# Even frequencies of a folded sequence transform split into four groups

## The chip, the cores and the metric

The program runs on one core of one Trainium2 chip. A core has several engines that run their own instruction streams and meet through semaphores: TensorE (PE: matmuls and transposes; PEld is its loading of weights), VectorE (DVE), ScalarE (ACT), GpSimd (POOL) and SyncE (SP, here the engine that issues most DMAs). Matmuls write PSUM banks; the other engines read these and return them. All data are fp32 unless said otherwise. The metric is the device time of one execution in microseconds, median of several; lower is better. A profiled execution is a separate one.

## What is computed

Four batches go through attention and then through a Fourier mixing block with an MLP:

```python
batch, n_heads, seq, head_dim = (4, 8, 768, 64)
# attention, per head
q_bucket = sum of 6 sign bits of q @ proj          # k_bucket likewise
scores = scale * q @ k^T, -1e9 where q_bucket != k_bucket
attn_out = softmax(scores) @ v
x = attn_out.transpose(0, 2, 1, 3).reshape(B, S, H * D)   # (4, 768, 512)
# Fourier mixing and MLP, per batch
X = fft(fft(x, axis=1), axis=2); mixed = real(X)
u = x + mixed
un = (u - mean(u)) / sqrt(var(u) + 1e-6)           # over the 512 channels
out = u + relu(un @ w_ch1) @ w_ch2                 # 512 -> 2048 -> 512
```

Only the real part of the two-dimensional transform over 768 positions and 512 channels is wanted, so cosines and sines are enough, and both can be halved by symmetry: adding and subtracting mirrored entries ("folding") separates even from odd frequencies, and cosine from sine terms.

## The kernel before

**Two interleaved generators.** `attention(b)` and `mix(b)` are Python generators. `mix` of batch b-1 is stepped inside `attention(b)`: after every attention step the main loop calls `next(other)` until the count of steps done keeps up with `(MIX - LEFT)` steps in all, spread over the 24 steps of attention (`while done * steps < (MIX - LEFT) * (i - wait)`, L1611). What is left of a mix runs ahead of the next attention; `mix(3)` runs alone at the end. By the profile `mix(0)` takes from about 130 to 350 us, `mix(1)` 350 to 610, `mix(2)` 610 to 870 and `mix(3)` 904 to the end. Only the first part of the program (up to the end of `attention(0)`) is emitted in a fixed order; afterwards the tile framework's scheduler decides the order of instructions on every engine, from priorities, program order and its own estimates of when operands are ready. Helpers bend it: `in_turn` and `done_by` tie an instruction behind the latest noted one of an engine, `behind` ties a matmul to the matmul before it and lifts it.

**Attention.** A pair of heads n (four pairs per batch) has six chunks c of 128 keys. Scores `sc` (L905, two 64-row matmuls of 384 columns per half g) go into two double-bank PSUM buffers ("sc"); ScalarE takes the exponential into one of two `pk` buffers (L916); VectorE multiplies `pk` by the mask "bucket of q equals bucket of k" (L930, from `qb` and `kb`); TensorE multiplies by values into `oo` (L941); VectorE adds `pk` into `acc` (L1037, 1536 columns, two chunks one after the other every second step), which is what is left of a chunk's `pk` besides `oo`. At the end of a pair `scale` sums `acc` over keys on TensorE (L951), spreads the reciprocals with eight small ScalarE copies (L984), a VectorE transpose (L989) and multiplies (L993), giving `x`. `prepare(n + 1)` makes `qt` and `kt` (VectorE transposes, L779), the bits (L836, L840) and `qb`, `kb` (L850, L860, evacuated at L535, L537 and L864), and `load` fetches q, k, v through SP.

**The transform in `mix`.** `fold` (L1110) works on a channel half `cp`: for each parity `pc` of channel frequencies it forms e = x of one half plus or minus x of the other (L1118, 768 columns), f = first plus or minus second half of the sequence for `par` 0 (even) and 1 (odd) sequence frequencies (L1123), and z, four additions of f to itself mirrored, for both `par` at once (L1132), with a copy of two special columns (L1136). z has 384 rows for each `par`, ordered cosine rows, both special ones, sine rows. `fold(b, 0)` runs inside `attention(b)`, in the last pair; `fold(b, 1)` begins `mix(b)`.

Then come six `cs` tiles (L1158), three of 128 rows for each `par`, which transform the channels: a tile takes only cosine or only sine channel products (256 or so columns in all, written to PSUM with stride 2 for the two `pc`), the middle tile both. ScalarE copies them into F (L1165, L1171, the latter mirrored). Then, per block j of 128 channels, the products A and B (L1187): for each `par`, `k` 0 and 1 (cosine into A, sine into B), two matmuls t accumulate over two 128-row tiles of F with the constant `sq` into 193 or 192 columns. VectorE adds or subtracts A and B to and from x in four additions of 384 columns (L1201), which return the two PSUM banks.

**The MLP in `mix`.** Both products run as seven-product (Strassen-like) schemes: sums t1, t2, t4, t3 of blocks of x (L1445, L1446, L1447, L1452) and of the weights; `un` transposes of x (L1213) for the residual and the norm; inner products `h_p` (L1467), with combinations of weights fetched through SP into a ring from `ad` (L1440); outer products `o` (L1346) with weights `bd` refetched by quarters (L1351), and VectorE additions from PSUM (L1358, L1392 to L1398). The weights' combinations `ad` and `bd` are written to DRAM during `mix(0)` (L1266, L1317), through SP. Results are stored at L1096.

**PSUM.** Besides the two double-bank "sc" and the two "o" buffers of attention there are two banks "ps". `pt` (L520) gives `mix` its banks: only those two, except at the start and once attention is over (`roomy`), when it also uses the "o" and "sc" buffers, six in all.

Of the kernel before, what the change touches and what calls it, by code (L numbers as in the profile page):

```python
# [49 lines left out]
def _consts():  # L50


    s = np.arange(HALF)
    freq = np.concatenate([2 * np.arange(NK), 2 * np.arange(NK) + 1])
    ang = 2.0 * np.pi * (np.outer(s, freq) % S) / S
    seq = np.stack([np.cos(ang), np.sin(ang)])
    seq = seq.reshape(2, NT // 2, P, 2 * NK).transpose(2, 0, 1, 3)


    d = np.arange(DM // 2)  # L60
    ang = 2.0 * np.pi * (np.outer(d, np.arange(DM)) % DM) / DM
    sin = -np.sin(ang)
    sin[0] = 1.0 - 2.0 * (np.arange(DM) % 2)
    chan = np.concatenate([np.cos(ang), sin]).reshape(NDC, P, DM).transpose(1, 0, 2)

    off = np.zeros((P, 2))
    for h in range(2):
        off[h * D : h * D + NBITS] = 0.5  # L70
        off[h * D + NBITS] = (NBITS / 4.0, -1.0)


    pw = np.zeros((P, 2, P))
    for r in range(P):
        h, bit = divmod(r % 32, NBITS)
        if h < 2:
            pw[r, h] = 2.0**bit


    d = np.arange(DM // 2)
    fr = np.concatenate([np.arange(DM // 2 + 1), np.arange(1, DM // 2)])
    ang = 2.0 * np.pi * (np.outer(d, fr) % DM) / DM
    ch = np.where(np.arange(DM) <= DM // 2, np.cos(ang), np.sin(ang))
    ch = ch.reshape(2, P, DM // 2, 2).transpose(1, 0, 3, 2)

    s = np.concatenate([np.arange(2, HALF // 2, 2), np.arange(1, HALF // 2, 2)])  # L90
    rows = np.concatenate([s, [0, HALF // 2], s])
    kind = np.repeat([0, 1, 2, 3], [len(s), 1, 1, len(s)])
    sq = np.zeros((2, 2, P, HALF + 1))
    for par in range(2):
        cols = slice(par * NK, HALF + 1 if par else NK)
        ang = 2.0 * np.pi * (np.outer(rows, freq[: HALF + 1][cols]) % S) / S
        for k in range(2):
            own = kind == (0 if par == k else 3)
            own |= (kind == 1) & (k == 0) | (kind == 2) & (k == par)
            w = np.where(own[:, None], np.sin(ang) if k else np.cos(ang), 0.0)  # L100
            w = w.reshape(NT // 2, P, -1)
            sq[0, k, :, cols] = w[0 if par == k else 2]
            sq[1, k, :, cols] = w[1]
    sq = sq.transpose(2, 0, 1, 3)
    return {
        "pw": np.ascontiguousarray(pw, dtype=np.float32),
        "ch": np.ascontiguousarray(ch, dtype=np.float32),
        "sq": np.ascontiguousarray(sq, dtype=np.float32),
        "seq": np.ascontiguousarray(seq, dtype=np.float32),
        "chan": np.ascontiguousarray(chan, dtype=np.float32),  # L110

        "off4": np.ascontiguousarray(np.tile(off[:32], (4, 1)), dtype=np.float32),
        "own": np.ascontiguousarray(
            np.where(np.arange(P)[:, None] // 32 % 2 == np.arange(2), BIG, 0.0),
            dtype=np.float32,
        ),
        "off": np.ascontiguousarray(off, dtype=np.float32),
    }
# [367 lines left out]
def _main(  # L486
# [616 lines left out]
    def turned(ap, first, n):  # L1103

        at = ap[tuple([slice(None)] * (len(ap.shape) - 1) + [slice(first, first + 1)])]
        return bass.AP(at.tensor, at.offset, [*[list(d) for d in at.ap[:-1]], [-1, n]])

    def fold(b, cp):


# [4 lines left out]
        for pc in range(2):  # L1115
            ef = wt([P, 2, S], F32, "ef", f"ef{b}_{cp}_{pc}", 1)
            e = ef[:, 0]
            nc.vector.tensor_tensor(  # L1118
                e, x[:, cp], x[:, cp + 2], op=ALU.subtract if pc else ALU.add
            )  # L1120
            f = ef[:, 1].rearrange("p (r n) -> p r n", r=2)
            for par in range(2):
                nc.vector.tensor_tensor(  # L1123
                    f[:, par], e[:, 0:HALF], e[:, HALF:S],
                    op=ALU.subtract if par else ALU.add,
                )
            z = zs[b][:, cp, pc]
            n = HALF // 4 - 1
            for at, op in ((0, ALU.add), (2 * n + 3, ALU.subtract)):

                for i, first, last in ((0, 1, n), (n, 2 * n + 2, n + 1)):
                    nc.vector.tensor_tensor(  # L1132
                        z[:, :, at + i : at + i + last], f[:, :, first : first + last],
                        turned(f, 2 * n + 1 if i == 0 else HALF - 1, last), op=op,
                    )
            nc.vector.tensor_copy(  # L1136
                z[:, :, 2 * n + 1 : 2 * n + 3], f[:, :, 0 : n + 2 : n + 1]
            )
            yield

    def mix(b):
# [5 lines left out]
        hd = DM // 2  # L1147
        F = wt([P, 2, 2, 2, DM], F32, "F", f"F{b}", 1)
        nc.gpsimd.memset(F[:, :, 1, :, 0 : hd + 1 : hd], 0.0)
        for par in range(2):  # L1150
            for t in range(NT // 2):
                ps = pt([P, DM], f"cs{b}_{par}_{t}")
                kinds = (0, 1) if t == 1 else (par ^ (t // 2),)
                for pc in range(2):
                    lo = 0 if 0 in kinds else hd // 2 + 1 - pc
                    hi = hd if 1 in kinds else hd // 2 + 1 - pc
                    for cp in range(2):
                        nc.tensor.matmul(  # L1158
                            ps[:, pc + 2 * lo : pc + 2 * hi - 1 : 2],
                            z[:, cp, pc, par, t * P : (t + 1) * P],  # L1160
                            ch[:, cp, pc, lo:hi], start=(cp == 0), stop=(cp == 1),
                        )
                f = F[:, par, :, t % 2]
                for k in kinds:
                    done_by[ET.Activation] = nc.scalar.copy(  # L1165
                        f[:, k, k : hd + 1 - k],
                        ps[:, k * (hd + 1) : DM if k else hd + 1],
                    )
                f = f[:, kinds[0] : kinds[-1] + 1, hd + 1 :]
                r = ps[:, (kinds[0] + 1) * hd - 1 : (kinds[0] + 1) * hd]  # L1170
                nc.scalar.copy(  # L1171
                    f,
                    bass.AP(
                        r.tensor, r.offset, [r.ap[0], [hd, len(kinds)], [-1, hd - 1]]
                    ),
                )
                yield

        for j in range(NDC):
            pa, pb = (pt([P, HALF + 1], f"{nm}{b}_{j}") for nm in "AB")
            for par in range(2):
                cols = slice(par * NK, HALF + 1 if par else NK)
                for k, ps in enumerate((pa, pb)):
                    for t in range(2):
                        nc.tensor.matmul(  # L1187
                            ps[:, cols], F[:, par, k, t, j * P : (j + 1) * P],
                            sq[:, t, k, cols], start=(t == 0), stop=(t == 1),
# [2 lines left out]
            for ps, op in (pa, ALU.add), (pb, ALU.subtract):  # L1192
                for i in range(2):
# [8 lines left out]
                        u, u, f, op=op if (j < 2) ^ i else ALU.add  # L1202
                    )
            yield

        yield from mlp7(b)

# [388 lines left out]
    for b in range(B):  # L1596
        if b > 0:
# [9 lines left out]
            for i, _ in enumerate(attention(b), 1):  # L1607
                if b == 1 and i == 2:
                    for f, avg in means:
                        centre(f, avg)  # L1610
                while done * steps < (MIX - LEFT) * (i - wait):  # L1611
                    next(other)
                    done += 1
        if b == B - 1:
# [75 lines left out]
```

## Time and profile before

| what | value |
| --- | --- |
| time, median of 3 runs | 1075.66 us (1075.48 to 1076.36) |
| profiled execution, its own time | 1079.48 us |
| span of the profiled execution | 1077.7 us, granted TensorE clock 0.994 of full |
| cs, groups in batches 1 to 3 | 3 tiles of 128 rows per `par` |
| A and B, even half, per batch | 16 matmuls of 193 columns, two records each |
| DMA | 103.13 MB, 96 GB/s over the span |

The profiled execution takes 3.8 us longer than the median of the others, so its parts are compared with its own time. The span runs from its first to its last instruction. The page gives busy time by engine over the whole span, the span in 40 slices, the chain of work that ended last, and groups of instructions by line, engine and operation. An fp32 matmul shows as two records, so "x4965" counts records. In a timeline line the columns are the start in us, the duration, engine, line, operation, output and inputs, shapes, how many in a row were joined, and in brackets the idle time ahead of it and what ended that. "Step" below is the time from one record's start to the next one's on the same engine while it is busy; it is shorter than a record's own duration, which overlaps with its neighbours.

### The profile page before, as it was taken

To read this page: it belongs to the slowest core of one execution; us is meant where nothing else is said; L and a number is where in the kernel's file an instruction comes from. 1 tells how busy PE (TensorE), PEld (TensorE's weight loads), DVE (VectorE), ACT (ScalarE), POOL (GpSimd) and SP (SyncE) were. 2 spreads that over 40 slices of the span, in tenths; PEclk is the share of its full clock that TensorE was granted. 3 is DMA by queue.
4 is the path that set the end of the run, shared out by engine and by line. 5 is a ranking of instruction groups with operands and counts; after the bars stand their busy time and mean duration, and the time that the engine had idled before them with its cause. 6 is when DMAs were issued, how large, how long until landed. Compare 5 with 4: busy or idle time off the path is not lost.

```text
span 1077.7 us, 14180 instructions
## 1 busy us (share of the span) xinstructions
PE 1037.1 (96%) x4965; PEld 634.2 (59%) x4965; DVE 779.9 (72%) x1328; ACT 500.0 (46%) x1055; POOL 59.1 (5%) x132
## 2 busy tenths in 40 slices
PE   7999899999999999999999999999999999999997
PEld 3333364447644585545664575645675579668576
DVE  5788969896799977777858876776856875644353
ACT  6888554662287414455335424454325522440420
POOL 0000000011000020010000020010000012100000
PEclk9999999999999999999999999999999999999999
DMA  8764551370154461224062233222033205222301
GB/s 202 202 139 88 103 140 48 122 231 15 26 131 170 135 180 45 52 64 88 10 191 75 64 102 118 50 65 69 15 112 94 69 23 173 60 79 91 124 20 42
DMA packets 175710, 103.13 MB, mean 96 GB/s; under 512 B 129552, under 2 KB 162960, under 8 KB 175632
## 3 DMA queue, kind: packets, MB, share of 16 engines
q1 hardware_dynamic: 169840, 88.65, 30.5%
q0 software_dynamic: 4224, 13.11, 3.9%
q8 instruction: 41, 0.67, 0.2%
q10 hardware_dynamic: 1568, 0.39, 0.2%
q14 instruction: 37, 0.30, 0.1%
HBM read 81.14 MB, written 20.97 MB: 95 GB/s over the span
## 4 chain that ended last, share of the span: by engine, by line
PE 77%; DVE 12%; ACT 6%; issue 2%; SPq 1%; DMA 1%; ACTq 0%; DVEq 0%
PE o L1346 26%; PE h_p L1467 22%; PE oo L941 10%; PE sc L905 9%; PE cs L1158 3%; ACT pk L916 2%; DVE pk L930 2%; PE A L1187 2%; DVE acc L1037 2%; PE B L1187 1%; PE sum L951 1%; SPq L576 1%; DVE x L1201 1%; PE bits L836 1%; DMA kn<-in_k_dram 1%
## 5 line engine op out<-in xcount | busy, mean ns | idle before, releaser
L1346 PE MATMUL o<-w,h 128*128 128x256 f32 x1152 | 260.1, 383 | 0.8 <-DVE w L1358 0.5
L1346 PEld LDWEIGHTS o<-w,h 128*128 128x128 f32 x1152 | 217.8, 191 | 41.7 <-issue 6.4
L916 ACT ACTIVATE pk<-sc 128x768 f32<-128x768 f32 x192 | 147.1, 807 | 80.0 <-PE oo L941 34.7
L1467 PE MATMUL h_p<-x,w 128*128 128x384 f32 x448 | 165.4, 497 | 3.1 <-ACT w L1534 1.7
L905 PE MATMUL sc<-qt,kt 64*128 64x384 f32 x768 | 153.9, 503 | 3.1 <-ACT pk L916 2.8
L930 DVE SCALAR_TENSOR_TENSOR pk<-qb,kb,pk 128x768 f32<-128x768 bf16 x132 | 128.7, 1012 | 38.4 <-ACT pk L916 38.3
L941 PE MATMUL oo<-pk,vn 128*64 128x385 f32 (+1 forms) x768 | 146.2, 495 | 0.8 <-DVE pk L930 0.6
L1467 PEld LDWEIGHTS h_p<-x,w 128*128 128x128 f32 x448 | 82.4, 190 | 69.3 <-issue 9.8
L1467 PE MATMUL h_p<-w 128*128 128x384 f32 x288 | 106.1, 490 | 0.1
L1037 DVE TENSOR_TENSOR acc<-acc,pk 128x1536 f32<-128x1536 f32 (+1 forms) x64 | 98.5, 1549 | 5.4 <-ACT pk L916 5.2
L941 PEld LDWEIGHTS oo<-pk,vn 128*64 128x64 f32 x768 | 50.5, 136 | 86.3 <-issue 72.8
L905 PEld LDWEIGHTS sc<-qt,kt 64*128 64x128 f32 x768 | 66.3, 186 | 55.9 <-issue 19.0
L1467 PEld LDWEIGHTS h_p<-w 128*128 128x128 f32 x288 | 53.6, 190 | 39.6 <-ACT w L1522 2.4
L1376 ACT COPY tq<-o 128x256 f32<-128x256 f32 x24 | 8.9, 372 | 105.0 <-PE o L1346 105.0
L1358 DVE SCALAR_TENSOR_TENSOR w<-o,rs,w 128x256 f32<-128x256 f32 x56 | 26.6, 479 | 41.2 <-PE o L1346 41.2
L1481 ACT ACTIVATE h<-h 128x384 f32<-128x384 f32 x72 | 37.4, 524 | 24.6 <-DVE h L1523 10.5
L1346 PE MATMUL o<-w 128*128 128x256 f32 x176 | 42.2, 383 | 0.2 <-DVE w L1358 0.2
L1518 DVE TENSOR_TENSOR h<-h 128x384 f32<-128x384 f32 x32 | 17.8, 555 | 29.7 <-ACT h L1517 29.7
L1096 POOL DMA_DIRECT2D out_dram<-w x30 | 16.3, 547 | 407.6 <-issue 314.6
L1346 PEld LDWEIGHTS o<-w 128*128 128x128 f32 x176 | 32.9, 190 | 7.5 <-DVE w L1358 1.2
L1365 ACT COPY tq<-o 128x256 f32<-128x256 f32 x24 | 8.8, 368 | 60.1 <-PE o L1346 59.9
L1392 DVE TENSOR_TENSOR tq<-tq,o 128x256 f32<-128x256 f32 x24 | 10.0, 417 | 36.4 <-PE o L1346 36.4
(169 smaller groups left out, 1317.4 us busy)
## 6 DMA issues: line engine op xcount, KB each, us to landing
w<-ad SPq DMA_DIRECT2D x168, 128.0 KB, 2.0
w<-bd SPq DMA_DIRECT2D x42, 512.0 KB, 4.4
zraw<-in_moe_w_ch_dram POOLq DMA_DIRECT2D x16, 512.0 KB, 3.9
bd<-w SPq DMA_DIRECT2D x14, 512.0 KB, 4.4
vn<-in_v_dram SPq DMA_DIRECT2D x32, 192.0 KB, 3.3
qn<-in_q_dram SPq DMA_DIRECT2D x120, 48.0 KB, 2.4
kn<-in_k_dram SPq DMA_DIRECT2D x60, 96.0 KB, 3.1
zraw<-in_moe_w_ch_dram SPq DMA_DIRECT2D x8, 512.0 KB, 6.9
```

The lines of the kernel that those rows point to most:

```text
L905: last[0] = nc.tensor.matmul(ps[:, h, 0:HALF], kt[rows, ks], qt[rows, qs], start=kb is not None, stop=True,)
L916: done_by[ET.Activation] = nc.scalar.activation(pk[:, g, :, 0:HALF], ps[:, :, 0:HALF], AF.Exp, scale=SCALE)
L930: done_by[ET.DVE] = nc.vector.scalar_tensor_tensor(w, qb[:, h].rearrange("p (g s) -> p g s", g=2), kb[:, h, c : c + 1], w, op0=ALU.is_equa ...
L941: oo = nc.tensor.matmul(oos[g][h * D : (h + 1) * D, 0:w], nat["v", n][:, (2 * c + h) * D : (2 * c + h + 1) * D], pk[:, g, h, 0:w], start=( ...
L1037: done_by[ET.DVE] = nc.vector.tensor_tensor(acc[:, g], (first if c == 1 else acc)[:, g], new[:, g], op=ALU.add,)
L1158: nc.tensor.matmul(ps[:, pc + 2 * lo : pc + 2 * hi - 1 : 2], z[:, cp, pc, par, t * P : (t + 1) * P], ch[:, cp, pc, lo:hi], start=(cp == 0) ...
L1187: nc.tensor.matmul(ps[:, cols], F[:, par, k, t, j * P : (j + 1) * P], sq[:, t, k, cols], start=(t == 0), stop=(t == 1),)
L1346: nc.tensor.matmul(ps, a[:, r], right7[i][:, r], start=start and r == 0, stop=r == HF // 2 - 1, skip_group_check=not start,)
L1358: nc.vector.scalar_tensor_tensor(t[:, cols], src, r, t[:, cols], op0=ALU.mult, op1=ALU.add)
L1467: nc.tensor.matmul(ps, left[:, k], right[i][:, k], start=start and k == 0, stop=k == 1, skip_group_check=not start,)
L1481: done_by[ET.Activation] = nc.scalar.activation(h, h, AF.Relu)
L1518: done_by[ET.DVE] = nc.vector.tensor_tensor(c22, c21, c22, op=ALU.add)
```

## The change

For batches 1 to 3 the even frequencies (`par` 0) are folded once more. Frequency 2m over 768 positions is frequency m over 384; these split again into even m and odd m. z for `par` 0 then consists of four groups of 97, 96, 96 and 95 rows, beginning at rows 0, Q + 1, 2Q + 1 and 3Q + 1 (Q = 96): cosine rows for even m and for odd m, sine rows for odd m and for even m. `refold` makes them from f in two VectorE additions of 384 columns, eight of 94 to 96 columns written through interleaved access patterns, and one small copy; the old fold then handles `par` 1 alone, with four additions and a copy of its own.

The `cs` tiles of `par` 0 become four, of 97, 96, 96 and 95 rows. None of them needs both kinds of channel products. In A and B, for `par` 0, each pair of accumulating 193-column matmuls becomes two single ones: group t has its own 97 or 96 frequencies, contracts over 95 to 97 rows, and writes every second column of the same 193 columns of PSUM. Odd frequencies and the VectorE additions at L1201 stay.

The constant for it, `sq2`, is loaded over the even columns of `sq` after batch 0's A and B, which still use the old one, by a DMA on SP. The step count of a mix rises by the extra tile: `MIX + (b > 1)`, the mix that attention(2) or attention(3) steps.

```diff
+    even, odd = 2 * np.arange(1, HALF // 8), 2 * np.arange(HALF // 8) + 1
+    pairs = np.concatenate([even, odd])
+    sq2 = np.zeros((P, 2, 2, NK))
+    for k, rest, rows in (
+        (0, 0, np.concatenate([[0], pairs, [HALF // 4]])),
+        (0, 1, np.concatenate([[0], pairs])),
+        (1, 1, np.concatenate([[HALF // 4], pairs])),
+        (1, 0, pairs),
+    ):
+        ang = 2.0 * np.pi * (np.outer(rows, np.arange(rest, NK, 2)) % HALF) / HALF
+        sq2[: len(rows), rest, k, : ang.shape[1]] = np.sin(ang) if k else np.cos(ang)
...
+    Q = HALF // 4
+
+    def refold(z, f, spare):
+
+        h = spare[:, 0:HALF].rearrange("p (s r n) -> p s r n", s=2, r=2)
+        g = f.rearrange("p (r h n) -> p h r n", r=2, h=2)
+        for i, op in ((0, ALU.add), (1, ALU.subtract)):
+            nc.vector.tensor_tensor(h[:, i], g[:, 0], g[:, 1], op=op)
+        for op, first, step in ((ALU.add, 1, 2 * Q + 1), (ALU.subtract, 3 * Q + 1, -2 * Q + 1)):
+            for r, i0, n in ((0, 1, Q // 2 - 1), (1, 0, Q // 2)):
+                a, d = h[:, 0, r, i0 : i0 + 1], first + (Q // 2 - 1) * r
+                d = z[:, d : d + 1]
+                nc.vector.tensor_tensor(
+                    bass.AP(d.tensor, d.offset, [list(d.ap[0]), [step, 2], [1, n]]),
+                    h[:, :, r, i0 : i0 + n],
+                    bass.AP(
+                        a.tensor, a.offset + Q - 1 - i0,
+                        [list(a.ap[0]), [2 * Q, 2], [-1, n]],
+                    ),
+                    op=op,
+                )
+        nc.vector.tensor_copy(
+            bass.AP(z.tensor, z.offset, [list(z.ap[0]), [Q + 1, 2], [Q, 2]]),
+            h[:, :, 0, 0 : Q // 2 + 1 : Q // 2],
+        )
...
+            if b > 0:
+                refold(z[:, 0], f[:, 0], e)
+                z, f = z[:, 1:2], f[:, 1:2]
...
+        tiles = [
+            (par, t * P, P, (0, 1) if t == 1 else (par ^ (t // 2),), t % 2)
+            for par in range(2) for t in range(NT // 2)
+        ]
+        if b > 0:
+            tiles[0:3] = (
+                (0, 0, Q + 1, (0,), 0), (0, Q + 1, Q, (0,), 1),
+                (0, 2 * Q + 1, Q, (1,), 1), (0, 3 * Q + 1, Q - 1, (1,), 0),
+            )
+        for t, (par, z0, m, kinds, slot) in enumerate(tiles):
+            ps = pt([P, DM], f"cs{b}_{par}_{t}")[0:m]
...
-                            z[:, cp, pc, par, t * P : (t + 1) * P],
+                        z[:, cp, pc, par, z0 : z0 + m],
...
+                        if b > 0 and par == 0:
+                            m = Q + 1 - t if k == 0 else Q - 1 + t
+                            nc.tensor.matmul(
+                                ps[:, t:NK:2], F[0:m, 0, k, t, j * P : (j + 1) * P],
+                                sq[0:m, t, k, 0 : Q + 1 - t], start=True, stop=True,
+                            )
+                            continue
                         nc.tensor.matmul(
                             ps[:, cols], F[:, par, k, t, j * P : (j + 1) * P],
                             sq[:, t, k, cols], start=(t == 0), stop=(t == 1),
...
+        if b == 0:
+            nc.sync.dma_start(sq[:, :, :, 0:NK], cn["sq2"].ap())
...
-                while done * steps < (MIX - LEFT) * (i - wait):
+                while done * steps < (MIX + (b > 1) - LEFT) * (i - wait):
```

More of the change, by code (lines that the diff above doesn't have):

```diff
@@ L108, in _consts @@
         "sq": np.ascontiguousarray(sq, dtype=np.float32),
+        "sq2": np.ascontiguousarray(sq2, dtype=np.float32),
         "seq": np.ascontiguousarray(seq, dtype=np.float32),
@@ L1149, in mix @@
         nc.gpsimd.memset(F[:, :, 1, :, 0 : hd + 1 : hd], 0.0)
[L1150 to L1159, printed above, removed]
-                            z[:, cp, pc, par, t * P : (t + 1) * P],
[L1161 to L1167, printed above, removed]
-                    )
[L1169 to L1175, printed above, removed]
-                )
-                yield
@@ new lines, in mix @@
+        tiles = [
[9 more added lines that the diff above has]
+            ps = pt([P, DM], f"cs{b}_{par}_{t}")[0:m]
+            for pc in range(2):
+                lo = 0 if 0 in kinds else hd // 2 + 1 - pc
+                hi = hd if 1 in kinds else hd // 2 + 1 - pc
+                for cp in range(2):
+                    nc.tensor.matmul(
+                        ps[:, pc + 2 * lo : pc + 2 * hi - 1 : 2],
+                        z[:, cp, pc, par, z0 : z0 + m],
+                        ch[:, cp, pc, lo:hi], start=(cp == 0), stop=(cp == 1),
+                    )
+            f = F[0:m, par, :, slot]
+            for k in kinds:
+                done_by[ET.Activation] = nc.scalar.copy(
+                    f[:, k, k : hd + 1 - k],
+                    ps[:, k * (hd + 1) : DM if k else hd + 1],
+                )
+            f = f[:, kinds[0] : kinds[-1] + 1, hd + 1 :]
+            r = ps[:, (kinds[0] + 1) * hd - 1 : (kinds[0] + 1) * hd]
+            nc.scalar.copy(
+                f,
+                bass.AP(
+                    r.tensor, r.offset, [r.ap[0], [hd, len(kinds)], [-1, hd - 1]]
+                ),
+            )
+            yield
@@ L1186, in mix @@
                     for t in range(2):
+                        if b > 0 and par == 0:
+                            m = Q + 1 - t if k == 0 else Q - 1 + t
+                            nc.tensor.matmul(
+                                ps[:, t:NK:2], F[0:m, 0, k, t, j * P : (j + 1) * P],
+                                sq[0:m, t, k, 0 : Q + 1 - t], start=True, stop=True,
+                            )
+                            continue
                         nc.tensor.matmul(
```

## The prediction

> **What bounds the kernel now.** I read the page's busy times, then the windows by stage, then the groups by form, then the timelines around the transform. Page, first part:
>
> ```profile
> PE 1037.1 (96%) x4965; PEld 634.2 (59%) x4965; DVE 779.9 (72%) x1328; ACT 500.0 (46%) x1055; POOL 59.1 (5%) x132
> ```
>
> TensorE works for 96% of the span. Of the 40.6 us without a matmul, some 24 lie in the first 130 us and the closing stores. So removed TensorE time is worth its full length, except where another engine releases TensorE. The windows (us, then PE, PEld, DVE, ACT, POOL busy) show where that is:
>
> ```profile
> 610.00:653.00 43.00, 43.00 (x206) 33.59 (x206) 30.96 (x63) 10.15 (x29) 7.12 (x15) 1.00 0.45 128
> 653.00:674.00 21.00, 20.73 (x124) 11.67 (x123) 16.79 (x19) 12.00 (x24) 1.60 (x3) 1.00 0.15 47
> 674.00:696.00 22.00, 19.83 (x121) 14.66 (x120) 15.69 (x26) 6.09 (x14) 0.00 (x0) 1.00 0.32 54
> 911.00:922.00 11.00, 11.00 (x72) 10.98 (x71) 7.41 (x15) 1.30 (x4) 0.00 (x0) 1.00 0.01 1
> ```
>
> 674 to 696 is the second half of batch 2's transform (products A and B, transposes `un`), run inside batch 3's attention: TensorE loses 2.17 us there. At 400 to 445 batch 1 does the same. 911 to 922 is batch 3's, which has no attention beside it: no loss. TensorE's own timeline shows the owner of the losses:
>
> ```profile
> 678.63 1.54 PE L1187 MATMUL A<-sq,F 128*128 128x193 f32 x8 [0.68 <-DVE x L1201]
> ...
> 689.63 1.54 PE L1187 MATMUL A<-sq,F 128*128 128x193 f32 x8 [0.55 <-DVE x L1201]
> ...
> 693.59 0.77 PE L1213 MATMUL un<-ident,x 128*128 128x128 f32 x5 [0.70 <-DVE x L1201]
> ```
>
> VectorE's four additions per channel block (L1201) return the PSUM banks of A and B. Batches 1 and 2 have two banks for this, batch 3 six. VectorE's timeline after them:
>
> ```profile
> 692.51 1.02 DVE L1201 TENSOR_TENSOR x<-x,B 128x384 f32<-128x384 f32 x2 [0.28 <-PE B L1187]
> 693.45 1.75 DVE L1037 TENSOR_TENSOR acc<-acc,pk 128x1536 f32<-128x1536 f32 x1
> 695.12 0.95 DVE L1446 TENSOR_TENSOR w<-x,w 128x768 f32<-128x768 f32 x1
> 695.98 1.75 DVE L1037 TENSOR_TENSOR acc<-acc,pk 128x1536 f32<-128x1536 f32 x1
> ```
>
> Every L1201 comes ahead of the two long sums L1037.
>
> [...] back-to-back 128-column loads of `cs` step 111 to 112 ns whether 127, 128 or 129 columns stream, against 162 ns for 192 or 193 and 216 for 256. [...] `cs` writes every second column and its 256 columns still step 216 ns, as the contiguous `o` products do. I price stride 2 at nothing.
>
> **The change part by part.**
>
> *A and B, even half.* Each fp32 matmul is two records. Per channel block 4 matmuls of 193 columns become 4 of 97 or 96: 8 x 162.5 = 1.30 us become 8 x 112 = 0.90. Gain 0.40 per block, 1.6 per batch, 4.8 over 12 blocks. [...]
>
> *cs.* Three tiles, 8 x 111.5 + 8 x 216 + 8 x 111.5 = 3.51 us, become four of 8 x 110 = 3.52 us: nothing. Each of the four is evacuated by two ScalarE copies (0.27 + 0.38 us and 0.2 us of signal) while the next runs 0.88 us on the second bank: up to 0.1 us twice in batches 1 and 2. The lone extra ACT copy per batch is covered by ScalarE's idle time (46% busy); uncovered it is 0.4.
>
> *Fold.* Of this the trace has the old form: L1132, 190 or 192 columns, steps 0.27 us; 384 steps 0.47. That gives 0.065 us plus N/0.96 each. Old tail per (channel half, parity): 4 x 0.27 + 0.07 = 1.15. New: 2 x 0.27 + 8 x 0.165 + 2 x 0.07 = 2.0. Plus 0.87, 3.5 us of VectorE per batch. In batches 2 and 3 it lies under `o` products; batch 3's z is complete at 893.3 against its first use at 904.28, 11 us of cover for 1.7. Without cover it would cost 3.5. Bounds on the unseen interleaved writes: 0.165 and twice that, 1.3 us more a batch, still covered.
>
> *The new constant's load* (395 KB, SP queue) waits until batch 0's A and B are read, at about 171; behind it stand the `ad` stores, used 240 us later. It needs the next quarter's buffers only microseconds later than now. Nothing[...].
>
> *Order, batch 1 before cs.* The compiled order puts batch 2's first scores behind the last `o` products. That removes these waits (ScalarE's 8 small copies stood ahead of the exponential):
>
> ```profile
> 372.77 0.92 PE L905 MATMUL sc<-qt,kt 64*128 64x384 f32 x4 [0.27 <-ACT pk L916]
> 375.27 0.97 PE L905 MATMUL sc<-qt,kt 64*128 64x384 f32 x4 [1.59 <-ACT pk L916]
> ```
>
> Minus 1.86. But VectorE is full from 350 to 376 (34.3 of 36 us). Walking it with the refold added, the L1358 that frees the next `o` bank stands behind L989, which waits for those 8 copies, and ends near 375.3, 1.0 us after TensorE wants the bank. Also 0.3 for a score wait and cs. Net -0.6. Some q and k loads move behind the seven `bd` loads; their users come 4 us or more later.
>
> *Order in A and B, batches 1 and 2.* Two things change. VectorE now has L1037, half of A3's additions, L1037, the other half, B3's: before, A3, B3, L1037. And TensorE has the next scores, the first `oo` group and the transposes interleaved ahead of the first MLP product. I walk batch 2 from its first A product (674.67 now), 0.2 us from matmul to addition and 0.15 back. VectorE: A0 and B0 done at 4.8, kt 5.8, A1 6.7, B1 11.1, A2 12.2, L1445 13.1, B2 14.0, L1037 15.7, L1037 again 17.9 (half of A3 between), A3 18.3, B3 19.3, then L930, L1446, L930 to 22.0 and, with L1447, the second chunk's to 24.7. TensorE: A0, qb, B0, kb, score, A1, score to 6.0, `oo` 8.7, B1 9.9, A2 11.0, B2 (0.27 lost) 12.4, A3 13.5, B3 (0.7 lost) 15.3. The next score needs a PSUM buffer that the exponential frees, which must wait for L1037 to finish with `pk`: 16.6, 1.3 lost. Transposes 18.4; `oo` waits for L930 until 22.1, 1.0 lost; MLP at 26.6. Now the same work, less the 9.4 us of MLP, sums and other transposes done by 711.3, takes 36.65 - 9.4 = 27.2. Batch 2 gains 0.6, less 0.2 for cs. In batch 1, A1's second half stands behind `oo`: 0.65 later, gain 0, less 0.2. Of 3.2 us that the two batches' matmuls save, 0.6 is left.
>
> *Batch 3.* TensorE 2.2 us per block, additions 1.9: still TensorE's. Copies of the last cs tile are 0.15 late. Gain 1.6, but L1445 and L1446, which the second MLP product needs, now follow all additions: ready at 12.25 from the first A product, TensorE there at 11.7. It stands at 13.7 now with 0.1 us less done: gain 1.5.
>
> Sum: batch 1 -0.6 - 0 + 0.2, batch 2 -0.4, batch 3 -1.5: -2.3. Profiled execution: 1079.48, of it 1077.7 span, so 1077.2. It stands 3.8 above the median of 1075.66[...]; the same difference on the median gives **1073.4**, 0.21% less.
>
> **Rivals.** *All of it arrives* (1069.5): 4.8, batch 1's 1.9 whole, minus 0.5. For it: 96% busy, and work pulled ahead in one stage leaves VectorE ahead in the next. Against: three of the four waits in the stage are VectorE's already. *VectorE takes over, slower* (1079): if the pair of L1037 ahead of B3's additions delays score and `oo` by 1.5 us more than walked in both batches, and the first fold in batch 1, on a full VectorE, passes its 1.7 us on, 3 + 1.7 - 2.3 + 0.9 of waits at moved qb copies gives +3.3. It decides once the losses of the stage, 2.2 now, exceed about 4.5 per batch. *The matmuls do not shorten* (1078): a short matmul costs 162 as before, and the added orders lose 2. Against: `cs` steps 112.
>
> **How the numbers follow.** The walked case 0.45, all of it 0.27, VectorE 0.2, no shortening 0.08. 0.2% (2.15 us) is about what a measurement of this kernel can tell from no change. The walk is good to 1.5 us: half of it falls beyond 0.2% faster. Faster 0.27 + 0.23 = 0.50; same 0.22 + 0.03 = 0.25; slower 0.25. The walked case alone 1071.9 to 1075.5; the range, 8 in 10, from all of it to the lighter half of VectorE's case: 1069.3 to 1078.6.
>
> **What would show it.** A and B records of 97 columns stepping 112 ns; 96 `z` additions of 94 to 96 columns at 0.25 us; no wait of 1.59 near 375; in batches 2 and 3's common stage, waits of about 1.3 (score, on an exponential behind L1037) and 1.0 (`oo`, on L930); batch 3's cs to first MLP product about 1.5 shorter. I am wrong if 97 columns step 82 or 160, if z holds up cs, or if those waits are absent or twice as long.

## The result, and the profile after

The changed kernel takes 1081.33 us (median of 6 runs, 1080.64 to 1082.82) against 1076.13 us before: a ratio of 1.0043, 95% interval 1.0032 to 1.0054. The forecast was 1073.4, with a range of 1069.3 to 1078.6. The time rose instead of falling.

TensorE's busy time fell, as the page's first part of the changed kernel shows, and VectorE's rose by about the 10 us that the new folds were costed at:

```profile
PE 1034.6 (96%) x4989; PEld 628.8 (58%) x4989; DVE 790.1 (73%) x1412; ACT 499.7 (46%) x1058; POOL 63.9 (6%) x132
```

The windows of the changed kernel (us, then PE, PEld, DVE, ACT, POOL busy, granted clock, DMA share, GB/s), first those that answer to the prediction's, then two of the MLP's second half of batches 1 and 2:

```profile
610.00:653.00 43.00, 43.00 (x206) 33.46 (x205) 32.36 (x77) 10.17 (x28) 7.16 (x15) 1.00 0.44 123
653.00:674.00 21.00, 20.73 (x132) 11.79 (x131) 16.73 (x19) 12.10 (x25) 1.56 (x3) 1.00 0.15 57
674.00:696.00 22.00, 20.35 (x123) 13.58 (x124) 18.32 (x29) 8.24 (x16) 0.00 (x0) 0.92 0.35 54
911.00:922.00 11.00, 11.00 (x83) 10.79 (x82) 5.15 (x11) 3.02 (x10) 0.54 (x1) 1.00 0.12 44
...
550.00:610.00 60.00, 58.77 (x238) 28.59 (x238) 45.70 (x81) 30.84 (x65) 0.00 (x0) 1.00 0.35 93
800.00:870.00 70.00, 68.65 (x288) 38.61 (x288) 49.83 (x90) 32.59 (x67) 0.00 (x0) 1.00 0.32 99
```

The last two, in the kernel before:

```profile
550.00:610.00 60.00, 59.95 (x251) 30.64 (x251) 45.03 (x69) 32.03 (x66) 0.00 (x0) 1.00 0.39 104
800.00:870.00 70.00, 69.95 (x290) 40.01 (x289) 50.61 (x79) 32.67 (x67) 0.44 (x1) 1.00 0.30 94
```

The common stage of batch 2 (674 to 696) has no more idle time than it had (1.65 us against 2.17), though its granted clock of 0.92 makes some records longer (the score pairs at 691.91 and 692.55 step 0.64 us, where 0.32 is usual). What is new is where TensorE had been fully busy: 1.2 us idle in 550 to 610 and 1.4 in 800 to 870, between MLP products. TensorE's timeline of the changed kernel names who was late:

```profile
574.62 1.56 PE L1526 MATMUL h_p<-x,w 128*128 128x384 f32 x4 [0.60 <-ACT h L1576]
...
594.33 1.56 PE L1526 MATMUL h_p<-w 128*128 128x384 f32 x4 [0.62 <-ACT w L1593]
...
689.03 0.66 PE L1238 MATMUL B<-sq,F 95*128 95x97 f32 x4 [0.46 <-DVE x L1257]
...
691.45 2.60 PE L918 MATMUL sc<-qt,kt 64*128 64x384 f32 x8 [1.09 <-ACT pk L929]
...
852.43 1.56 PE L1526 MATMUL h_p<-w 128*128 128x384 f32 x4 [1.30 <-ACT w L1593]
```

The waits at 689 and 691 are those that the prediction walked to (VectorE on a bank, then a score on an exponential). Those at 574, 594 and 852 are ScalarE's copies of `h_p` that return MLP banks, and nothing in the prediction stands for them. VectorE in the common stage has the walked order: half of A3's additions (L1257, L1201 of before) between the two long sums into acc (L1050, L1037 of before), the other half behind the second, and B3's last:

```profile
688.80 1.75 DVE L1050 TENSOR_TENSOR acc<-acc,pk 128x1536 f32<-128x1536 f32 x1
690.47 0.54 DVE L1257 TENSOR_TENSOR x<-x,A 128x384 f32<-128x384 f32 x1
690.94 1.75 DVE L1050 TENSOR_TENSOR acc<-acc,pk 128x1536 f32<-128x1536 f32 x1
692.61 0.54 DVE L1257 TENSOR_TENSOR x<-x,A 128x384 f32<-128x384 f32 x1
693.07 1.00 DVE L1257 TENSOR_TENSOR x<-x,B 128x384 f32<-128x384 f32 x2
```

For where the time went, the trace is cut at each batch's first A product. The three stretches behind batch 1's first A product hold all the rest of the kernel; times in us, from the traces of all kernels that ran, the ratio with its 95% interval. "Idle" is TensorE's idle time in the first and the second stretch. "Shapes" counts, in the same two, how often TensorE goes over to a stationary operand of another shape: 64 rows for scores, 64 columns for `oo`, 32 rows or columns for `qb`, `kb`, `bits` and `sum`, 95 to 128 of both for the transform and the MLP.

| kernel | A of 1 to A of 2 | A of 2 to A of 3 | A of 3 to last matmul | idle | shapes | ratio to before |
| --- | --- | --- | --- | --- | --- | --- |
| before | 254.73 | 236.63 | 158.76 | 2.96, 2.70 | 84, 67 | |
| changed | 259.24 | 239.84 | 156.34 | 5.86, 4.50 | 88, 67 | 1.0043 (1.0032 to 1.0054) |
| e1, step count undone | 255.49 | 236.87 | 156.34 | 4.82, 4.55 | 79, 61 | 0.9978 (0.9967 to 0.9989) |
| e2, step count alone | 257.44 | 236.91 | 158.75 | 5.35, 3.78 | 83, 64 | 1.0027 (1.0019 to 1.0034) |
| e3, VectorE's fold alone | 256.25 | 238.17 | 158.75 | 4.02, 3.75 | 84, 67 | 1.0016 (1.0009 to 1.0023) |
| e4, batch 3 alone | 254.71 | 238.40 | 156.34 | 2.96, 3.81 | 84, 67 | 0.9988 (0.9977 to 0.9999) |
| e5, e1 with GpSimd | 255.56 | 236.93 | 156.34 | 4.82, 4.55 | 79, 61 | 1.0008 (1.0000 to 1.0016) |
| e6, short matmuls alone | 252.52 | 234.42 | 157.10 | 2.39, 2.12 | 84, 67 | 0.9949 (0.9934 to 0.9964) |
| e7, batches 2 and 3 | 257.07 | 236.88 | 157.10 | 4.07, 4.56 | 86, 61 | 1.0018 (1.0011 to 1.0025) |
| e8, one step fewer than e1 | 256.36 | 237.76 | 156.34 | 4.82, 4.56 | 81, 63 | 1.0007 (0.9999 to 1.0015) |
| e9, steps aligned | 254.41 | 236.21 | 156.34 | 3.70, 3.43 | 84, 67 | 0.9959 (0.9945 to 0.9973) |
| e10, e9 with GpSimd | 256.94 | 237.29 | 156.34 | 4.76, 4.50 | 84, 67 | 0.9995 (0.9987 to 1.0004) |
| e11, e9, half the fold later | 253.35 | 234.97 | 156.34 | 2.44, 2.11 | 86, 69 | 0.9948 (0.9935 to 0.9962) |
| e12, e9, all of it later | 256.77 | 236.18 | 156.34 | 4.51, 2.90 | 84, 69 | 0.9977 (0.9971 to 0.9984) |

So the change gains 2.42 us in batch 3 and loses 4.51 and 3.21 in the two batches before: +5.3, the size of the measured 5.2. In the traced execution of before the granted clock fell to 0.5 in two stretches of 3.4 us, from 205.3 and from 376.0. e4's code is the same up to batch 1's first A product but for line numbers; its trace has no such stretch and is 3.35 us ahead at that mark (416.59 against 419.94). That is most of the 3.8 us by which the profiled execution stood above the median. Against e4, the changed kernel is 0.6 us shorter from batch 0's first A product to batch 1's (266.6 against 267.2). Other traces have one such stretch too: e5 from 205.1, e10 from 590.7, e12 from 606.9 (in the last two it is worth up to 1.7 us of their first column, half of e4's difference), and the changed kernel from 691.8, where it seems to have cost little, since two executions of it at a granted clock of 0.999 took 1081.24 and 1081.49.

### The profile page after: what moved, and what is told of

It is laid out like the page before. It is cut to its first block, busy times and chain, and to the rows that moved or that the text cites. A ratio compares the mean times of both kernels' runs of the same rounds, so it can differ in the third digit from the quotient of the medians.

```text
span 1079.1 us, 14329 instructions
## 1 busy us (share of the span) xinstructions
PE 1034.6 (96%) x4989; PEld 628.8 (58%) x4989; DVE 790.1 (73%) x1412; ACT 499.7 (46%) x1058; POOL 63.9 (6%) x132
## 4 chain that ended last, share of the span: by engine, by line
PE 73%; DVE 15%; ACT 6%; issue 2%; DMA 1%; SPq 1%; DVEq 0%; ACTq 0%
PE o L1405 25%; PE h_p L1526 20%; PE oo L954 10%; PE sc L918 9%; PE cs L1207 3%; DVE pk L943 3%; DVE acc L1050 2%; ACT pk L929 2%; PE sum L964 1%; PE A L1243 1%; ACT rr L997 1%; PE un L1272 1%; PE B L1243 1%; DVE x L1257 1%; DMA kn<-in_k_dram 1%
## 5 line engine op out<-in xcount | busy, mean ns | idle before, releaser
L1526 PE MATMUL h_p<-x,w 128*128 128x384 f32 x448 | 164.1, 493 | 4.4 <-ACT h L1566 1.8
L954 PE MATMUL oo<-pk,vn 128*64 128x385 f32 (+1 forms) x768 | 149.0, 496 | 1.6 <-DVE pk L943 1.3
L1526 PEld LDWEIGHTS h_p<-x,w 128*128 128x128 f32 x448 | 82.2, 190 | 70.5 <-issue 8.1
L1526 PE MATMUL h_p<-w 128*128 128x384 f32 x288 | 106.4, 490 | 2.0 <-ACT w L1593 1.9
L1050 DVE TENSOR_TENSOR acc<-acc,pk 128x1536 f32<-128x1536 f32 (+1 forms) x64 | 98.5, 1548 | 5.4 <-ACT pk L929 5.2
L1526 PEld LDWEIGHTS h_p<-w 128*128 128x128 f32 x288 | 53.3, 190 | 41.2 <-ACT w L1593 4.4
L1417 DVE SCALAR_TENSOR_TENSOR w<-o,rs,w 128x256 f32<-128x256 f32 x56 | 26.5, 478 | 36.4 <-PE o L1405 36.4
```

The source lines that it names most:

```text
L954: oo = nc.tensor.matmul(oos[g][h * D : (h + 1) * D, 0:w], nat["v", n][:, (2 * c + h) * D : (2 * c + h + 1) * D], pk[:, g, h, 0:w], start=( ...
L1050: done_by[ET.DVE] = nc.vector.tensor_tensor(acc[:, g], (first if c == 1 else acc)[:, g], new[:, g], op=ALU.add,)
L1417: nc.vector.scalar_tensor_tensor(t[:, cols], src, r, t[:, cols], op0=ALU.mult, op1=ALU.add)
L1526: nc.tensor.matmul(ps, left[:, k], right[i][:, k], start=start and k == 0, stop=k == 1, skip_group_check=not start,)
```

## The experiments

Two theories stood against each other: that the shift of attention against the mix (one more step, `MIX + (b > 1)`) puts attention's work where the MLP can't bear it ("order"), and that refold's added VectorE time delays the MLP ("VectorE").

**e1, the step count undone.**

```diff
-                while done * steps < (MIX + (b > 1) - LEFT) * (i - wait):
+                while done * steps < (MIX - LEFT) * (i - wait):
```

> The changed kernel with one line undone: the mix's step count stays at MIX, so that attention(2) and attention(3) step it as before. Between the two traces, TensorE's dips in clock taken out, the changed kernel loses about 2.3 us in the MLP of batch 1 (509 to 570) and 1.8 in that of batch 2 (825 to 904). Theory 'order': the added step moves attention's pieces against the MLP's, and ScalarE and VectorE serve them too late; without it the 4.1 us come back: 1081.3 - 4.1 = 1077.2. Theory 'VectorE': refold's 3.5 us of VectorE time a batch, half of it in the last pair of each attention, delays the MLP's additions: 1081.3 stays.

1074.63 us: 6.7 below the changed kernel, below the kernel before, and the largest effect of any single line here. 3.75 and 2.97 us come back in the two stretches. "Order" was right in sign and too small, and lateness of ScalarE and VectorE is only a part of it: TensorE's idle time falls by 1.04 us in the first stretch and not at all in the second. What else falls is the number of changes of shape, 88 to 79 and 67 to 61. One costs some 0.2 us without any wait: in the changed kernel's trace `h_p` records step 0.32 us, the last one ahead of a score group (the four from 316.17) 0.42, and the first pair of scores behind it (317.55) 0.43 where later pairs step 0.32. The trace of before has the same steps. By that estimate the changes are worth 1.8 and 1.2 us. In the second stretch the lower clock from 691.8 also makes records of the changed kernel 1.6 us longer, partly in place of waits.

**e2, the step count alone on the kernel before.**

```diff
-                while done * steps < (MIX - LEFT) * (i - wait):
+                while done * steps < (MIX + (b > 1) - LEFT) * (i - wait):
```

> The kernel before with nothing but the step count MIX + (b > 1). Theory 'order': 4 us slower, 1080.2. Theory 'VectorE': no change, 1076.1 (within 1).

1079.35 us, 3.0 slower with the computation untouched; 2.7 of it between the A products of batches 1 and 2. VectorE's timeline of e2 in that batch's last pair shows how:

```profile
586.69 1.16 DVE L1132 TENSOR_TENSOR z<-ef 128x190 f32<-128x190 f32 x4
...
587.84 1.94 DVE L930 SCALAR_TENSOR_TENSOR pk<-qb,kb,pk 128x768 f32<-128x768 bf16 x2
589.70 0.55 DVE L1518 TENSOR_TENSOR h<-h 128x384 f32<-128x384 f32 x1
590.36 0.56 DVE L1523 TENSOR_TENSOR h<-h,w 128x384 f32<-128x384 f32 x1
```

and TensorE's of e2 what it costs:

```profile
591.89 1.56 PE L1467 MATMUL h_p<-x,w 128*128 128x384 f32 x4 [1.52 <-ACT h L1526]
```

The fold of the next transform and the masks of two chunks stand ahead of the MLP's additions to h on VectorE. The relu on ScalarE waits for the addition, the copy at L1526 stands behind that relu, and the copy holds one of the mix's two banks. The first chunk's masks stand between the fold's parts, at 584.25. One step more or less decides whether this row of work meets the MLP's products or not.

**e3, VectorE's fold alone.** Nothing else of the change.

```diff
+            for i, op in ((0, ALU.add), (1, ALU.subtract)) if b > 0 else ():
+                nc.vector.tensor_tensor(
+                    e[:, i * HALF // 2 : (i + 1) * HALF // 2],
+                    f[:, 0, 0 : HALF // 2], f[:, 0, HALF // 2 : HALF], op=op,
+                )
...
+                    for zr, fr in ((z[:, 0:1], f[:, 0:1]), (z[:, 1:2], f[:, 1:2])) if b > 0 else ((z, f),):
```

> The kernel before with the changed kernel's VectorE work alone in the folds of batches 1 to 3: the fold's four additions and copy made for each par apart (eight of 95 or 96 columns, two copies), and two additions of 192 columns into a spare that nothing reads. Transform, matmuls and step count as before. Theory 'VectorE': slower by what the MLP stages lose, 1076.1 + 4.1 = 1080.2, or more where batch 1's first fold meets a full VectorE. Theory 'order': within 1 of 1076.1.

1078.37 us, 2.1 slower: half of what "VectorE" said. Each of the two stretches is 1.5 us longer, with the same kind of wait as e2 (1.05 us at 590.71, on the copy at L1541, which is L1534 of before). Ahead of batch 1's first A product it gains 1.1 instead: the longer first fold of batch 1 brought the reordering of that place, in which the wait of 1.59 us near 375 is gone. Both theories are true in part, and they name the same place.

**e4, the change for batch 3 alone.**

```diff
-            if b > 0:
+            if b >= 3:
                 refold(z[:, 0], f[:, 0], e)
...
-        if b == 0:
+        if b == 2:
             nc.sync.dma_start(sq[:, :, :, 0:NK], cn["sq2"].ap())
```

> The change for batch 3 alone (refold, four tiles, single matmuls; the constant loaded after batch 2's A and B; step count as before). Between the traces batch 3 from its cs to the end is 2.4 us shorter. Theory 'order': only that, 1076.1 - 2.4 = 1073.7. Theory 'VectorE': refold in attention(3)'s last pair costs 1.8 of it, 1075.5.

1075.94 us, within the interval 0.1 to 2.5 us faster. By its trace 1.77 us are lost in attention(3)'s last pair (1.30 of it in one wait at 847.53, on the copy at L1593, as in the changed kernel) and 2.42 gained behind batch 3's first A product: "VectorE", with numbers that fit.

**e5, GpSimd in place of VectorE.**

```diff
-                nc.vector.tensor_tensor(
+                eng.tensor_tensor(
...
-                refold(z[:, 0], f[:, 0], e)
+                refold(z[:, 0], f[:, 0], e, nc.vector if cp else nc.gpsimd)
```

> The changed kernel with MIX undone (e1), and refold's additions of 94 to 96 columns for the first channel half (cp 0, run in each attention's last pair) issued on GpSimd instead of VectorE. Of the 1.74 us that the new fold adds to VectorE there, 8 x 0.165 = 1.3 us leave it. Theory 'VectorE's time in the last pair': e3's loss of 1.54 us in each of batches 2 and 3 comes back by three quarters, 1074.6 - 2.3 = 1072.3. Theory 'place': it was the shift of instructions, not their time, or GpSimd slows VectorE: 1074.6 or more.

1077.7 us, 3 above e1. The two stretches are e1's to 0.1 us, so nothing comes back; batch 1's first A product is some 2 us later than e1's, the lower clock from 205.1 taken out (waits of 0.5 to 1.1 between 356 and 374). In e1's alignment the last pair has no such wait (the one wait there, 0.46 us at 571.06, is on another copy), so e5 could not show a gain; e10 asks again where there is one.

**e6, the short matmuls alone.**

```diff
+                        if b > 0 and par == 0:
+                            m = 97 - t if k == 0 else 95 + t
+                            nc.tensor.matmul(
+                                ps[:, t:NK:2], F[0:m, 0, k, t, j * P : (j + 1) * P],
+                                sq[0:m, t, k, 0 : 97 - t], start=True, stop=True,
+                            )
+                            continue
```

> The kernel before with the short matmuls alone: A and B of the even half as single matmuls of 97 or 96 columns over 95 to 97 rows, written with stride 2, on the old z, F and sq (so the even half is not the transform's; everything else is as before). TensorE's work falls 3 x 1.6 = 4.8 us. Theory 'the additions at L1201 take it in batches 1 and 2' (two banks): 1.6 in batch 3 and under 0.5 in each of the others, 1076.3 - 2.2 = 1074.1. Theory 'all of it arrives': 1071.5.

1070.8 us, 5.3 faster (6.1 by the three stretches): all 4.8 us of TensorE arrive, and a little more. "All of it arrives" holds for the short matmuls as such, in batches 1 and 2 too (2.2 us in each stretch). With the steps of before, two banks and VectorE's additions leave these waits in TensorE's timeline of e6 in batch 2's common stage, 1.24 us where before had 1.93:

```profile
682.99 0.66 PE L1189 MATMUL B<-sq,F 95*128 95x97 f32 x4 [0.46 <-DVE x L1208]
...
685.43 0.77 PE L1220 MATMUL un<-ident,x 128*128 128x128 f32 x5 [0.78 <-DVE x L1208]
```

**e7, the change for batches 2 and 3, step count undone.** As e4 with 2 and 1 in place of 3 and 2, and MIX as before.

> The change for batches 2 and 3 with MIX undone (the constant loaded after batch 1's A and B). Against e1 it leaves out batch 1's part. By e1's trace batch 1's A reaches the place of before (+0.1) and its transform stage gives 0.8: so 1074.6 + 0.7 = 1075.3. If batch 1's first fold on a full VectorE costs anything, below e1: under 1074.6.

1078.81 us: 4.2 above e1, where 0.7 was expected. Its three stretches are 2.4 us longer than e1's, 1.6 of it in the first: with batch 1 as before, attention(2)'s last pair has the wait again (1.29 us at 592.60), which e1 has not. Leaving batch 1's part out was put at 0.7; it costs 1.6, and 0.8 more in batch 3, whose stretch is e6's. More of its executions than of e1's ran at a lower granted clock (mean 0.9970 against 0.9976); those at 0.998 or more have medians of 1077.5 and 1074.6, 2.9 apart. Some 0.5 us of that stay unexplained.

**e8, one step fewer.**

```diff
-                while done * steps < (MIX + (b > 1) - LEFT) * (i - wait):
+                while done * steps < (MIX - (b > 1) - LEFT) * (i - wait):
```

> The changed kernel with MIX - (b > 1) in place of MIX + (b > 1): two steps fewer than changed, one fewer than e1. Theory 'more of the mix per step of attention is worse, fewer is better': below e1 by some us, about 1070. Theory 'each count is another arrangement of both, with no direction': anywhere from 1073 to 1081, as e1, the change and e2 span it.

1076.81 us, between e1 and the changed kernel. Fewer steps are not better as such. Both stretches are 0.9 us longer than e1's with the same idle time to 0.01 us; two more changes of shape in each are worth about half of that. So the count has no direction, only alignment. That asks for the alignment of before, which neither e1 nor e8 has: with seven `cs` tiles a mix has one yield more than the loop was written for, so behind its even tiles it lies one step behind attention, whatever MIX is. e1's trace still has the scores among A and B, with the waits of the changed kernel's batch 1.

**e9, the steps aligned.** The yield behind the second of the four even tiles is left out, so that a mix has as many steps as before; MIX as before.

```diff
-            yield
+            if b == 0 or t != 1:
+                yield
...
-                while done * steps < (MIX + (b > 1) - LEFT) * (i - wait):
+                while done * steps < (MIX - LEFT) * (i - wait):
```

> The changed kernel with the mix's step count kept in both places: MIX as before, and no yield after the second of the four even tiles, so that a mix has as many steps as before. Everything of the transform is the change's. Theory 'step alignment': the MLP's and attention's pieces fall as in the kernel before, and what is left is e6's gain and e3's cost: 1076.1 - 5.3 + 2.1 = 1072.9. If the new order inside the A and B stage (kept here: qb, kb and scores between A and B) eats the short matmuls in batches 1 and 2, as the prediction walked it, 2.6 us less: 1075.5.

1072.31 us, 4.0 below before and 9.0 below the changed kernel, with every instruction of the change's transform in it. In the traced order of TensorE's groups (some 410, records of one tile in a row joined) e9 differs from before in 15 entries, the changed kernel in 50 and e1 in 59. The common stage of batch 2 has e6's waits (0.46 and 0.78), not the changed kernel's. What is left against e6 is mainly the last pair. VectorE's timeline of e9:

```profile
585.15 0.42 DVE L1133 TENSOR_TENSOR z<-ef 128x94 f32<-128x94 f32 x2
...
585.96 1.94 DVE L943 SCALAR_TENSOR_TENSOR pk<-qb,kb,pk 128x768 f32<-128x768 bf16 x2
587.82 0.56 DVE L1583 TENSOR_TENSOR h<-h,w 128x384 f32<-128x384 f32 x1
```

and TensorE's:

```profile
589.82 1.56 PE L1527 MATMUL h_p<-w 128*128 128x384 f32 x4 [1.31 <-ACT w L1594]
```

VectorE is busy from the fold through the masks to L1583, without a gap; L1594 on ScalarE follows a relu that needs L1583.

**e10, e9 with GpSimd in batches 2 and 3.** The edit of e5, for `b` 2 and 3.

> e9 with refold's additions of 94 to 96 columns of the first channel half on GpSimd in batches 2 and 3. Here the last pair has the order of before, in which e3 lost 1.54 us a batch. Theory 'VectorE's time': three quarters of it comes back, 2.3 below e9. Theory 'GpSimd slows VectorE, or place': as e9 or above.

1076.42 us, 4.1 above e9 (1.8 among the two and three executions at a granted clock of 0.998 or more, 1074.6 against 1072.9). The wait grew from 1.31 to 2.37 us in attention(2)'s last pair, and as much in attention(3)'s. VectorE's timeline of e10 says why:

```profile
579.57 0.17 DVE L1142 COPY z<-ef 128x4 f32<-128x4 f32 x1 [0.74 <-POOL z L1133]
...
584.78 0.17 DVE L1142 COPY z<-ef 128x4 f32<-128x4 f32 x1 [0.73 <-POOL z L1133]
...
584.93 3.80 DVE L943 SCALAR_TENSOR_TENSOR pk<-qb,kb,pk 128x768 f32<-128x768 bf16 x4
588.64 0.55 DVE L1583 TENSOR_TENSOR h<-h,w 128x384 f32<-128x384 f32 x1
```

The small copy behind the additions writes the same z and waits for GpSimd, 0.74 us each time, and then the masks of both chunks stand ahead of L1583 in one row of 3.80 us. A new wait took the place of the work. So e10 does not settle whether VectorE's time was the cause; taking the fold out of the way on VectorE itself does.

**e11 and e12, the fold later.** In batches 2 and 3 the second part of the first fold (e11), or both parts (e12), is tied behind the latest noted instructions.

```diff
-                    next(half, None)
+                    with in_turn() if b > 1 and c == 4 else nullcontext():
+                        next(half, None)
```

(e12 without `and c == 4`.)

> e9 with the second part (pc 1) of the first fold of batches 2 and 3 tied behind the latest noted instruction of each engine at the place where it is emitted. On VectorE it moves from ahead of the masks and the additions to h at L1582 and L1586 to behind them, among the first sums of the outer products. Theory 'the fold delays those additions': the waits of 1.31 at 589.82 and 1.30 at 844.23 on the copy at L1594 go, 2 x 1.4 back: 1072.3 - 2.8 = 1069.5. Theory 'it only moves': the outer products' sums are late by as much, 1072.3.

> The same with both parts of that fold tied so, pc 0 behind the first additions too. Theory 'the fold delays those additions': nothing left to gain over e11, 1069.5 or a little more where the fold meets the outer products' sums. Theory 'it only moves': 1072.3 or more.

e11 takes 1070.75 us, 0.9948 of before: the fastest version here of the whole computation, and faster than both kernels. The waits at 589.82 and 844.23 are gone, 1.1 and 1.2 us shorter stretches against 1.4 each expected. The intervals of e9 and e11 overlap; executions at a granted clock of 0.998 or more have medians of 1072.9 and 1070.6, 2.3 apart, as the two stretches together. VectorE's timeline of e11 at the same place has the masks without a fold among them, waiting for their exponentials, and L1584 (e9's L1583) 1.8 us sooner, counted from each kernel's first A product of batch 1 (e11's is 0.6 earlier):

```profile
580.73 1.95 DVE L943 SCALAR_TENSOR_TENSOR pk<-qb,kb,pk 128x768 f32<-128x768 bf16 x2 [1.36 <-ACT pk L929]
583.55 1.95 DVE L943 SCALAR_TENSOR_TENSOR pk<-qb,kb,pk 128x768 f32<-128x768 bf16 x2 [0.87 <-ACT pk L929]
585.41 0.55 DVE L1584 TENSOR_TENSOR h<-h,w 128x384 f32<-128x384 f32 x1
```

e12 overdoes it: 1075.29 us (1073.2 at a granted clock of 0.998 or more). There the fold's second part begins among the additions to h (L1158 at 603.62, ahead of L1588), a relu on ScalarE waits for L1588, and ScalarE's half of the evacuation of `qb` (L550) stands behind that relu. TensorE's timeline of e12 has this wait instead, in batch 1's stretch, and two of 0.42 and 0.20 us on exponentials near 857 in batch 2's:

```profile
606.34 0.24 PE L873 MATMUL kb<-pw,bt 32*128 32x2 bf16 x6 [1.86 <-ACT qb L550]
```

e12's second stretch is as long as e9's (236.18 against 236.21): "it only moves" is true of e12 and false of e11.

## Why the prediction was wrong

**The prices were right.** Of the eight records of A and B of 97 or 96 columns in a block, seven step 110 to 113 ns; the first, behind 192-column ones, steps 87, and the first 192-column one behind the eight 191 in place of 163. Together that is 0.9 us, as predicted; a block in batch 3 takes 2.20 us against 2.61. The page's groups by form show the new additions at the predicted size, here two of the changed kernel's on VectorE (count, busy us, mean ns, idle before):

```profile
L1133 DVE TENSOR_TENSOR z<-ef 128x96 f32<-128x96 f32 x24 | 6.0, 250 | 0.0
L1174 DVE TENSOR_TENSOR z<-ef 128x95 f32<-128x95 f32 x24 | 6.0, 248 | 0.0
```

The four small `cs` tiles take 3.49 us against 3.52 predicted. Stride 2 in PSUM shows no cost: 256 columns with it step 216 ns, as contiguous `o` products do. TensorE shows no wait for the load of `sq2`.

Three readings in the prediction were less firm than they look. That 97 columns step 112 ns was the author's estimate, and `cs` before could not show it: by the prediction's own steps a column takes (216 - 162) / 64 = 0.84 ns, so that 128 of them would take 108 by their number alone. The changed kernel shows it, with 110 to 113 ns where 96 columns would step some 81 by the same count; what sets those 110 ns no run shows. "From 350 to 376 (34.3 of 36 us)" is the window from 340; 350 to 376 has 24.65 of 26. And the fold's terms give 0.85, not 0.87, with four additions of 94 or 96 columns in `refold`, four of 95 or 96 in the old fold for `par` 1, and two first additions of 192 columns, where "The change" has eight and 384; VectorE's busy time rose by 3.4 us a batch.

**Batch 1 before its first A product** came to -0.6 us (against e4), near the -0.4 forecast (-0.6 walked, and 0.2 for cs): the wait of 1.59 us is gone, and one of 0.64 us at 372.48 (an `o` bank, behind L1417) stands in its place, with 0.44 at a `cs` tile.

**The step "Order in A and B, batches 1 and 2"** walked to the first MLP product, 26.6 us behind batch 2's first A product. It starts at 701.51, 26.75 behind 674.76. The waits were named rightly and a little too long: score 1.09 in batch 2 (0.91 in batch 1) against 1.3, `oo` 0.77 in batch 1 and none shown in batch 2 against 1.0. In batch 2 the lower clock from 691.8 lies inside the walk: records there are 1.6 us longer than in batch 1, which fills the place of the wait on `oo`, so some of that match is luck; batch 1, without it, takes 27.0 us to its first MLP product.

What failed is the step after the walk: the sum closed at the first MLP product, as if the rest of the batch ran as before. The extra tile's yield, which moved the scores into the common stage (e1 has them there, e9 has not), and the count raised for it moved the later pieces of attention against the MLP, and there the loss was made: e1 shows 3.75 and 2.97 us for the count and e9 another 1.1 and 0.7 for the yield, where the prediction had 0. Against before, TensorE's idle time is 2.9 us longer in the changed kernel's first stretch and 1.8 in its second; against e1 it is 1.0 and 0, and changes of shape weigh more. The prediction had no term for either.

**The step "Fold"** had the right 3.5 us a batch and the wrong cover. "In batches 2 and 3 it lies under `o` products" holds for the second channel half, which begins the mix. The first half runs in the last pair of attention, among the MLP's `h_p` products, where VectorE's additions to h release banks through ScalarE. e3 prices it at 1.5 us in each of two batches, and e11, which moves half of it, gets 1.1 and 1.2 back.

**Batch 3** was mis-sized: -1.5 predicted, -2.42 measured. 1.66 are the matmuls (e6 has them alone: 158.76 to 157.10). In the other 0.8 the first MLP product starts 9.4 us behind the first A product instead of 12.4, ahead of most transposes, and the wait of 0.41 us at the first bank of `un` is gone. The prediction kept the old order there.

**The rivals.** "VectorE takes over, slower" had the right side and, by luck, nearly the right time (1079), but not the mechanism: the pair of L1037 ahead of B3's additions cost what was walked, and its other part, batch 1's first fold on a full VectorE, brought a gain in e3. "All of it arrives" describes e6, that is, the change without its steps and folds. "The matmuls do not shorten" is refuted. Nothing in the forecast stood for the windows 550 to 610 and 800 to 870, where TensorE's new idle time shows most: the profile before had them 99.9% busy on TensorE, and VectorE in 578 to 593 for 14.89 of 15 us, a schedule with no slack for more of VectorE's work.

**The base.** The 3.8 us between profiled execution and median were taken as a fixed difference; mostly they were the two stretches of lower clock (3.35 us against e4), and the profiled executions of e6 and e7 stand 1.1 and 1.6 us below their medians. Subtracting them was right all the same.

**Open.** How the 3.2 us of batch 2's stretch in the changed kernel divide between its waits, its changes of shape and its stretch of lower clock, and the last 0.5 us of e7. That a step costs time through waits and changes of shape is read from the traces; no run removed one wait of the changed kernel, or one change of shape, by itself.

## What to carry to other kernels

Where two streams of work are interleaved by counted steps, a new step is an edit to the whole schedule: keep the number of steps first, then judge the saving (here the same transform was 5 us slower or 4 faster with one yield and one count). Look at TensorE's changes of shape beside its idle time: about 0.2 us each in these traces, they are counted as busy. Walk a moved order to the end of the stage that is interleaved with it, not to its first product. When work is added to an engine off the critical path, ask at each place where it runs which bank or buffer that engine is about to release, and if need be order it behind that.

## What was not expected of the hardware

The granted clock fell to 0.5 for 3.4 us once or twice in some executions, and cost up to 1.7 us each time, by an estimate from before's two (3.35 us against e4); a stage table has to be read with that in mind. In before's stretch from 376.0 `o` records step 0.43 us, where 0.22 is usual. In these traces it does not fall just anywhere. TensorE in the traced execution of before (us, busy, granted clock, DMA share, GB/s):

```profile
201.80:205.30 3.50, 1.78 (x11) 1.00 0.00 0
205.30:208.70 3.40, 3.40 (x9) 0.50 0.65 207
...
372.60:376.00 3.40, 1.64 (x8) 1.00 0.52 146
376.00:379.40 3.40, 3.40 (x10) 0.50 0.73 117
```

Each of the six such stretches inside the traced kernels begins right behind a spell in which TensorE was partly idle: it was busy for 1.85 of 3.4 us in the changed kernel ahead of 691.8, 1.54 in e12 (its wait of 1.86 taken off), 1.03 in e10 (its wait of 2.37 taken off), and e5 has 8.29 us of 10 in 200 to 210, as before has 8.28. Such a spell is not always followed by one: the changed kernel has 1.69 of 3.4 ahead of 205.3 and keeps a granted clock of 1.00 in the next 3.4 us. 11 of e10's 13 executions ran below a granted clock of 0.998 against 3 of e1's 10; that its longer wait causes the fall, and so costs TensorE more than its own length, is not shown.

An idle time shown ahead of a matmul can understate the loss: in the changed kernel the group at 852.43 starts 2.76 us behind the one before it, where such groups stand 1.29 apart, a loss of 1.47 against 1.30 shown, because a record (0.49 us) is longer than the step to the next (0.32). GpSimd's additions of 94 and 96 columns took 0.43 and 0.39 us on average in e10, against VectorE's 0.25; in e5 eight of them kept it busy for 5.3 us in each of the last two attentions' last pairs, 0.66 each. Beside them in e10 VectorE's four additions at L1174 took 1.13 us from first to last (from 577.70), where four of 0.25 that step 0.17, as in e9, take 0.76. In e10 it was mainly the wait of VectorE for GpSimd that cost the time.
